# Gated linear attention into two expert layers: the attention output computed turned, with heads on the partitions

## The chip, the cores and the metric

One core of a Trainium2 chip. The metric is the time of one execution on the device, in microseconds (us). The kernel before takes 953.18 us, the median of three runs (951.75 to 960.41).

## What is computed

```python
f = 1.0 / (1.0 + np.exp(-f_logit))
for t in range(S):
    state = f[:, :, t, :, None] * state + np.einsum('bhd,bhe->bhde', k[:, :, t], v[:, :, t])
    y[:, :, t] = np.einsum('bhd,bhde->bhe', q[:, :, t], state)
```

B = 4 sequences, H = 8 heads, S = 768 tokens, D = 48 columns a head. The 3072 tokens with their 384 columns then go through a mixture of 8 experts, of which each token takes two by noisy logits (`x @ w_gate` and `x @ w_noise`), and through a dense layer of 2048 columns with `h - tanh(h)`.

## The kernel before, in words

The attention is done by chunks of 128 tokens, 24 of them: chunk j is part c = j // 4 of sequence b = j % 4. The state of a sequence (`st`, L296) is carried from chunk to chunk, so chunks 0 to 3 have none yet. The loop at the end of the attention part runs over the chunks, and a chunk's work is spread over three turns of it: gates are made three chunks ahead (`decay`), scaled keys and queries two ahead (`scaled`), scores one ahead (`scores`). The order on each engine is the order of the code: `tc.manual_schedule()` is on.

- `scaled` (L314) raises e to the summed log gates for k (`epos`, in SBUF) and to their negative for q (`eneg`), and multiplies: k on the vector engine (DVE, L323), q on GpSimd (POOL, L325). Columns of two heads lie on 128 partitions, 64 a head, four pairs side by side.
- `scores` (L330) multiplies keys and queries on the tensor engine (PE), one head on 64 rows of the array, two heads in turn (`pA`), and DVE masks them into `am`.
- `outputs` (L357) makes the chunk's output with tokens on the partitions: q stationary and the state streaming (L364, 96 columns), scores stationary and v streaming (L366, 48 columns), into `pY`. ScalarE (ACT) copies it twice, as f32 and as scaled f16, and DVE makes the f16 rest.
- `key_rows` (L344) turns keys to rows (`pkr`); `states` (L375) makes the chunk's part of the state (`pK`) and adds it in.
- `x_transposed` (L394) turns the output over (`pE`, three transposes) for `logits` (L406), which multiplies it with 96 columns that begin with the 16 gate and noise columns (`pt`), chunk by chunk.
- `route` (L415) picks experts and slots for a group of four chunks (the last groups: 20 to 22, and 23 alone). It is a generator, `advance` runs it step by step between other work. `post` scatters rows of `xkeep` into the experts' slots in DRAM (`xs`) by GpSimd DMAs.

An f32 product is two passes over the array, each with its own weight load. Behind the loop the experts' products follow (`ph` L185, `py` L200), f16 in two parts, and the dense layer. They aren't touched by the change. The first block of expert 0 starts inside the last turn of the loop; its second block needs all rows scattered.

Of the kernel before, what the change touches and what calls it, by code (L numbers as in the profile page):

```python
# [22 lines left out]
NCH = S // 128  # L23
NT = B * NCH
CAP = 832
GN = 3 * 16 + NT * NE
# [45 lines left out]
def fast(ctx, tc, flag, f_cols, kq_cols, v_rows, gates, blank, w12, w_in, w_out, out):  # L72
# [49 lines left out]
    pre = consts.tile([128, NT + 1, NE], BF, name="pre")  # L122
# [127 lines left out]
    with ExitStack() as actx:  # L250
# [35 lines left out]
        wgn = gn[:, 0:48].rearrange("p (a c) -> p a c", a=3)  # L286
        nz = gn[:, 48:].rearrange("p (c b e) -> p c b e", c=NCH, b=B)
# [69 lines left out]
        def outputs(j):  # L357
            c, b = divmod(j, B)
            am, qT, vt = T.pop(("am", j)), T.pop(("qT", j)), T["v", j]
            pY = ps.tile([128, 512], F32, name="pY", tag="b5")  # L360
            for a in range(4):
                at = 96 * a
                if c:
                    nc.tensor.matmul(pY[:, at:at + 96], qT[:, a, :], st[b][:, at:at + 96], start=True, stop=False)  # L364
                for s in range(2):
                    nc.tensor.matmul(pY[:, at + 48 * s:at + 48 * s + 48], am[:, s, a, :], vt[:, 2 * a + s, :],  # L366
                                     start=not c, stop=bool(s) or not c)
            x = work.tile([128, DM], F32, name="x")
            nc.scalar.activation(x, pY[:, :384], AF.Copy)
            x16 = xkeep[j // 4 % 3][:, j % 4, :]  # L370
            nc.scalar.activation(x16[:, :DM], pY[:, :384], AF.Copy, scale=SX)
            nc.vector.scalar_tensor_tensor(x16[:, DM:], x, SX, x16[:, :DM], op0=OP.mult, op1=OP.subtract)
            T["x", j], T["x16", j] = x, x16

        def states(j):  # L375
            c, b = divmod(j, B)
            vt = T.pop(("v", j))
            if c == NCH - 1:
                return
            k = T.pop(("krows", j))  # L380
            pK = ps.tile([128, 4, 96], F32, name="pK", tag="b6")
            for a in range(4):
                nc.tensor.matmul(pK[:, a, :], k[:, a, :], vt[:, 2 * a:2 * a + 2, :].rearrange("p h d -> p (h d)"),  # L383
                                 start=True, stop=True)
            tsum = work.tile([128, 4, 96], F32, name="tsum")
            if c:
                nc.vector.tensor_tensor(tsum, pK, st[b][:, :384].rearrange("p (a d) -> p a d", a=4), op=OP.add)
            else:
                nc.vector.tensor_copy(tsum, pK)
            nc.gpsimd.tensor_tensor(st[b][:, :384].rearrange("p (a s d) -> p a s d", a=4, s=2),  # L390
                                    tsum.rearrange("p a (s d) -> p a s d", s=2),
                                    gall[:, j, :, :, None].to_broadcast([128, 4, 2, D]), op=OP.mult)
# [22 lines left out]
        def route(g):  # L415
# [25 lines left out]
            for _ in range(2 if g < len(groups) - 2 else 1):  # L441
                yield
            pos = ps.tile([128, 4, NE], F32, name="pt", tag="b7" if g > 4 else "b2")[:, :G]
            nc.tensor.matmul(pos, before, sel[:, jj], start=True, stop=False)
            nc.tensor.matmul(pos, ones, pre[:, jj], start=False, stop=True)
# [60 lines left out]
        for j in range(NT):  # L506
# [24 lines left out]
            x_transposed(j)  # L531
# [3 lines left out]
            if 4 <= j < 20 and not j % 2:  # L535
                split_weights(0, (j - 4) // 2)
        moe_first(*moe_steps[1])
        advance(20)
        post(8)
        logits(NT - 1)  # L540
        chains.append(route(len(groups) - 1))
# [204 lines left out]
    def checks():  # L746
# [9 lines left out]
        nc.tensor.matmul(count[:, 0], ones, pre[:, NT], start=True, stop=True)  # L756
        nc.tensor.matmul(count[:, 1], ones, pre[:, EARLY], start=True, stop=True)
        nc.tensor.matmul(count[:, 2], ones, pre[:, 4], start=True, stop=True)
# [316 lines left out]
def packed_rows(q, k, v, f_logit, w_gate, w_noise, noise, w1, w2):  # L1075
# [11 lines left out]
    gates = np.empty((128, GN), w_gate.dtype)  # L1087
    wgn = gates[:, 0:48].reshape(128, 3, 16)
    wgn[:, :, 0:8] = w_gate.reshape(3, 128, NE).transpose(1, 0, 2)
    wgn[:, :, 8:16] = w_noise.reshape(3, 128, NE).transpose(1, 0, 2)  # L1090
    gates[:, 0:48] = wgn.reshape(128, 48)
    gates[:, 48:] = noise.reshape(B, NCH, 128, NE).transpose(2, 1, 0, 3).reshape(128, NT * NE)
# [30 lines left out]
```

## Time and profile before

| | |
|---|---|
| median of three runs | 953.18 us |
| the profiled execution | 957.17 us |
| its span | 955.4 us |
| mean granted clock of PE | 0.995 of 2.4 GHz |
| PE busy | 940.5 us |
| DVE / ACT / POOL busy | 607.8 / 610.8 / 156.7 us |

The attention loop takes about the first 158 us of the span. Times in the rows are us from the span's start unless marked ns. PE is the product itself, PEld its weight load, which may run beside another product. A row of a timeline gives start, length, engine, line, operation, out<-in, shape and count; in brackets stands the time that the engine was idle before, and who ended it. Ends of products are modelled, so prices are better read from starts.

### The profile page before, as it was taken

Reading aid. Unit: us, or ns where it says so; the run is one execution under the profiler, and the core shown is the slowest. Engines: PE = TensorE matmul, PEld = TensorE weight load, DVE = VectorE, ACT = ScalarE, POOL = GpSimd, SP = SyncE. Lnnn points to the kernel's source line nnn. Section 1 sums busy time; section 2 is a strip of 40 time slices with the busy share of each in tenths; the row PEclk is TensorE's granted clock in tenths of the full one; section 3 lists DMA queues with packets and bytes.
Section 4 is the critical chain, followed back from the end, with each engine's and each line's share of the span. In section 5 each row is a group of like instructions: output and inputs, shape, how many; then the busy total and the mean of one; then the engine's idle time right before and its main releaser. Section 6 shows DMA issues by size and latency. Waiting matters only on the chain.

```text
span 955.4 us, 16329 instructions
## 1 busy us (share of the span) xinstructions
PE 940.5 (98%) x5970; PEld 581.3 (61%) x5970; DVE 607.8 (64%) x1274; ACT 610.8 (64%) x1593; POOL 156.7 (16%) x194
## 2 busy tenths in 40 slices
PE   8999999999999999999999999999999999999996
PEld 8999987555656565555556554555555555555553
DVE  7999995366565556566666655656566565665664
ACT  6777763475757566585858556666666666666653
POOL 2377785200000000000000035200301101000000
PEclk9999998999999999999999999999999999999999
DMA  7877754675464646564554376202222121110001
GB/s 274 282 246 262 251 181 141 179 203 175 139 172 134 186 138 196 138 171 127 153 139 128 95 182 141 67 25 51 75 49 51 34 59 42 42 26 1 34 1 38
DMA packets 111802, 120.04 MB, mean 126 GB/s; under 512 B 66400, under 2 KB 89568, under 8 KB 111584
## 3 DMA queue, kind: packets, MB, share of 16 engines
q1 hardware_dynamic: 105280, 99.63, 36.2%
q0 software_dynamic: 6144, 18.88, 6.4%
q8 instruction: 49, 0.80, 0.4%
q14 instruction: 41, 0.34, 0.1%
q10 hardware_dynamic: 288, 0.39, 0.1%
HBM read 76.41 MB, written 29.88 MB: 111 GB/s over the span
## 4 chain that ended last, share of the span: by engine, by line
PE 94%; DVE 2%; issue 1%; ACT 1%; DMA 1%; POOL 1%; SPq 0%; DVEq 0%; POOLq 0%; ACTq 0%
PE py L200 40%; PE ph L185 39%; PE pY L366 4%; PE pA L339 2%; PE pY L364 2%; PE pK L383 2%; PE pt L410 2%; PE pkr L352 1%; PE pK L492 1%; POOL xs L479 1%; PE pE L398 1%; DMA xt<-xs 0%; DMA xs<-xkeep,yslot 0%; DVE am L341 0%; DVE fc L312 0%
## 5 line engine op out<-in xcount | busy, mean ns | idle before, releaser
L200 PE MATMUL py<-wsplit,hs 128*128 128x384 f16 x2432 | 431.9, 326 | 1.0 <-DVE hs L650 0.8
L200 PEld LDWEIGHTS <-hs 128*128 128x128 f16 x2432 | 237.6, 98 | 172.4 <-DVE hs L650 1.5
L185 PE MATMUL ph<-xt,wsplit 128*128 128x512 f16 (+3 forms) x1152 | 224.4, 340 | 0.8 <-DMA xt<-xs 0.8
L185 PE MATMUL ph<-xt,winS 128*128 128x512 f16 x864 | 201.6, 379 | 0.0
L185 PEld LDWEIGHTS <-wsplit 128*128 128x128 f16 x1152 | 113.0, 98 | 87.6 <-DMA xt<-xs 1.2
L641 DVE SCALAR_TENSOR_TENSOR s<-s,z 128x512 f32<-128x512 f32 x96 | 66.4, 692 | 143.1 <-ACT s L638 142.0
L218 DVE SCALAR_TENSOR_TENSOR hs<-ph,hs 128x256 f16<-128x256 f32 (+2 forms) x192 | 79.7, 443 | 119.3 <-ACT hs L210 112.8
L210 ACT ACTIVATE hs<-ph 128x512 f16<-128x512 f32 (+3 forms) x128 | 65.8, 514 | 133.3 <-PE ph L185 125.3
L608 POOL DMA_INDIRECT g<-y_rows,yslot x48 | 47.8, 996 | 579.4 <-ACT wsplit L144 375.7
L637 ACT ACTIVATE z<-ph 128x512 f32<-128x512 f32 x96 | 57.2, 596 | 131.3 <-PE ph L185 131.3
L185 PEld LDWEIGHTS <-winS 128*128 128x128 f16 x864 | 84.5, 98 | 91.9
L145 DVE SCALAR_TENSOR_TENSOR wsplit<-raw,wsplit 128x768 f16<-128x768 f32 x72 | 70.3, 976 | 16.7 <-ACT wsplit L144 15.5
L149 ACT ACTIVATE junk<-wsplit 128x384 f16<-128x384 f16 x144 | 74.4, 517 | 2.3
L638 ACT ACTIVATE s<-z,bias_a 128x512 f32<-128x512 f32 x96 | 69.3, 722 | 3.1
L643 DVE SCALAR_TENSOR_TENSOR g<-s,ph 128x512 f32<-128x512 f32 x96 | 65.9, 687 | 3.3
L650 DVE TENSOR_TENSOR hs<-g,hs 128x512 f16<-128x512 f32 x96 | 65.7, 684 | 0.1
L144 ACT ACTIVATE wsplit<-raw 128x768 f16<-128x768 f32 x72 | 59.9, 832 | 1.3 <-DMA raw<-wo_f 1.3
L649 ACT ACTIVATE hs<-g 128x512 f16<-128x512 f32 x96 | 58.9, 613 | 1.1 <-DVE g L643 1.1
L479 POOL DMA_INDIRECT xs<-xkeep,yslot x48 | 56.1, 1169 | 18.8 <-issue 9.1
L366 PE MATMUL pY<-v,am 128*128 128x48 f32 x384 | 55.0, 272 | 0.0
L366 PEld LDWEIGHTS pY<-v,am 128*128 128x128 f32 x384 | 51.4, 198 | 0.1
L325 POOL TENSOR_TENSOR kqT<-eneg,kq 128x512 f32<-128x512 f32 x23 | 32.6, 1419 | 16.7 <-ACT eneg L321 16.4
(135 smaller groups left out, 910.1 us busy)
## 6 DMA issues: line engine op xcount, KB each, us to landing
raw<-in_w SPq DMA_DIRECT2D x64, 384.0 KB
kq<-in_kq_cols SPq DMA_DIRECT2D x24, 512.0 KB
y_rows<-yo SPq DMA_DIRECT2D x47, 192.0 KB
f<-in_f_cols SPq DMA_DIRECT2D x24, 256.0 KB
w<-in_moe_w_out SPq DMA_DIRECT2D x32, 192.0 KB
w<-in_moe_w_in SPq DMA_DIRECT2D x24, 256.0 KB
v<-in_v_rows SPq DMA_DIRECT2D x24, 192.0 KB
out<-o SPq DMA_DIRECT2D x22, 192.0 KB
```

The source lines that it names most:

```text
L145: nc.vector.scalar_tensor_tensor(t[:, 1], raw, SW, t[:, 0], op0=OP.mult, op1=OP.subtract)
L149: nc.scalar.activation(junk[:, :DM], RING[e, f][:, 0, 3 * i:3 * i + 3, :].rearrange("p a b -> p (a b)"), AF.Square, accum_out=wsum[:, 8 * ...
L185: nc.tensor.matmul(ph[:, :n], l, x[:, r, :n], start=(o == 0), stop=(o == 8))
L200: nc.tensor.matmul(p[:max(m, 128)], l, r, start=(f == 0 and o == 0), stop=(f == last and o == len(ops) - 1))
L210: nc.scalar.activation(hs[:, :n], ph[:, :n], AF.Relu, accum_out=hacc[:, at:at + 1])
L218: nc.vector.scalar_tensor_tensor(hs[:, at:at + hi - lo], ph[:, lo:hi], 0.0, hs[:, lo:hi], op0=OP.max, op1=OP.subtract)
L366: nc.tensor.matmul(pY[:, at + 48 * s:at + 48 * s + 48], am[:, s, a, :], vt[:, 2 * a + s, :], start=not c, stop=bool(s) or not c)
L479: sc = nc.gpsimd.indirect_dma_start(out=xs, out_offset=bass.IndirectOffsetOnAxis(ap=yslot[:, r, j:j + 1], axis=0), in_=T["x16", j], in_off ...
L638: nc.scalar.activation(s, z, AF.Square, scale=1.0 / SZ, bias=bias_a)
L641: nc.vector.scalar_tensor_tensor(s, s, ZD, z, op0=OP.add, op1=OP.mult)
L643: nc.vector.scalar_tensor_tensor(g, s, 0.5, ph, op0=OP.mult, op1=OP.mult)
L650: nc.vector.tensor_tensor(hs[:, 512:], g, hs[:, :512], op=OP.subtract)
```

## The change

The output of a chunk is made with heads' columns on the partitions and tokens in the free dimension: the state and v are stationary, q and the masked scores stream. The state gets 64 columns a head, with zeros behind the 48, so that the output of a pair of heads fills the partitions in the same padded layout as q. The products of v write 48 partitions, from 0 or from 64. ACT copies the turned output once, into a tile for the group's four chunks; four transposes turn it back to rows, which are split to f16 in the next turn. The logits of a group are one product: 16 gate columns stationary, 512 tokens streaming, and four small transposes bring them to rows. In the last group (one chunk) they are made as before. The counts for the slots are kept per group, and the product that makes slots adds up the chunks of a group. e to the gates for k is written to PSUM.

```diff
-GN = 3 * 16 + NT * NE
+GN = 4 * 16 + NT * NE
...
-        wgn = gn[:, 0:48].rearrange("p (a c) -> p a c", a=3)
+        wgn = gn[:, 0:64].rearrange("p (a c) -> p a c", a=4)
...
-        st = [acst.tile([128, 432], F32, name=f"st{b}") for b in range(B)]
+        st = [acst.tile([128, 4, 2, 64], F32, name=f"st{b}") for b in range(B)]
         for s_ in st:
-            nc.vector.memset(s_[:, 384:], 0.0)
+            nc.gpsimd.memset(s_, 0.0)
...
-            epos = work.tile([128, 512], F32, name="epos", bufs=1)
+            epos = ps.tile([128, 512], F32, name="epos", tag="b2")
...
         def outputs(j):
-            pY = ps.tile([128, 512], F32, name="pY", tag="b5")
+            pY = ps.tile([128, 4, 128], F32, name="pY", tag="b5")
+            if not c:
+                nc.tensor.matmul(pY, none, ones[:, None, :].to_broadcast([128, 4, 128]), start=True, stop=False)
+            else:
+                for a in range(4):
+                    nc.tensor.matmul(pY[:, a, :], st[b][:, a].rearrange("p s d -> p (s d)"), qT[:, a, :], start=(a == 0),
+                                     stop=False)
             for a in range(4):
-                at = 96 * a
-                if c:
-                    nc.tensor.matmul(pY[:, at:at + 96], qT[:, a, :], st[b][:, at:at + 96], start=True, stop=False)
                 for s in range(2):
-                    nc.tensor.matmul(pY[:, at + 48 * s:at + 48 * s + 48], am[:, s, a, :], vt[:, 2 * a + s, :],
-                                     start=not c, stop=bool(s) or not c)
-            x = work.tile([128, DM], F32, name="x")
-            nc.scalar.activation(x, pY[:, :384], AF.Copy)
-            x16 = xkeep[j // 4 % 3][:, j % 4, :]
-            nc.scalar.activation(x16[:, :DM], pY[:, :384], AF.Copy, scale=SX)
-            nc.vector.scalar_tensor_tensor(x16[:, DM:], x, SX, x16[:, :DM], op0=OP.mult, op1=OP.subtract)
-            T["x", j], T["x16", j] = x, x16
+                    nc.tensor.matmul(pY[64 * s:64 * s + D, a, :], vt[:, 2 * a + s, :], am[:, s, a, :], start=False,
+                                     stop=(a == 3))
+            g = group_of[j]
+            if j == groups[g][0]:
+                T["yT", g] = work.tile([128, 4, 4, 128], F32, name="yT")
+            nc.scalar.activation(T["yT", g][:, :, j - groups[g][0], :], pY, AF.Copy)
...
-        def x_transposed(j):
-            x = T.pop(("x", j))
-            p = ps.tile([128, 3, 128], F32, name="pE", tag="b0")
-            for a in range(3):
-                nc.tensor.transpose(p[:, a, :], x[:, a * 128:(a + 1) * 128], ident)
-            xT = work.tile([128, 3, 128], F32, name="xT", bufs=1)
-            nc.scalar.activation(xT, p, AF.Copy)
-            T["xT", j] = xT
+        def x_rows(j):
+            g = group_of[j]
+            p = T["pX", j] = ps.tile([128, 4, 128], F32, name="pX", tag="b0")
+            for a in range(4):
+                nc.tensor.transpose(p[:, a, :], T["yT", g][:, a, j - groups[g][0], :], ident)
+
+        def x_split(j):
+            p = T.pop(("pX", j)).rearrange("p a (s d) -> p (a s) d", s=2)[:, :, :D]
+            x16 = T["x16", j] = xkeep[j // 4 % 3][:, j % 4, :]
+            hi, lo = (x16[:, i * DM:(i + 1) * DM].rearrange("p (h d) -> p h d", h=H) for i in range(2))
+            nc.scalar.activation(hi, p, AF.Copy, scale=SX)
+            nc.vector.scalar_tensor_tensor(lo, p, SX, hi, op0=OP.mult, op1=OP.subtract)
...
-        def logits(j):
+        def logits(g):
+            y = T["yT", g]
             p = ps.tile([128, 96], F32, name="pt", tag="b7")
-            xT = T.pop(("xT", j))
-            for a in range(3):
-                nc.tensor.matmul(p, xT[:, a, :], gn[:, 16 * a:16 * a + 96], start=(a == 0), stop=(a == 2))
-            nc.scalar.activation(lgs[:, j, :], p[:, :16], AF.Copy)
+            for a in range(4):
+                nc.tensor.matmul(p, y[:, a, 0, :], gn[:, 16 * a:16 * a + 96], start=(a == 0), stop=(a == 3))
+            nc.scalar.activation(lgs[:, groups[g][0], :], p[:, :16], AF.Copy)
+
+        def group_logits(g):
+            G = len(groups[g])
+            p = ps.tile([16, 4, 128], F32, name="pt", tag="b7")
+            for a in range(4):
+                nc.tensor.matmul(p[:, :G], wgn[:, a, :], T["yT", g][:, a, :G, :], start=(a == 0), stop=(a == 3))
+            t = T["lgT", g] = work.tile([16, 4, 128], F32, name="lgT", bufs=1)
+            nc.scalar.activation(t[:, :G], p[:, :G], AF.Copy)
+
+        def group_rows(g):
...
+            for i in range(G):
+                nc.tensor.transpose(p[:, i, :], t[:, i, :], ident[:16, :16])
+            nc.scalar.activation(lgs[:, j0:j0 + G, :], p[:, :G], AF.Copy)
...
-            for j in js:
+            yield
+            if G > 1:
+                own_sum = small.tile([128, NE], BF, name="own_sum")
...
+                    nc.vector.tensor_reduce(own_sum, sel[:, jj].rearrange("p g e -> p e g"), axis=AX.X, op=OP.add)
...
+            tt(pre[:, g + 1], pre[:, g], own_sum, op=OP.add)
+            for _ in range(5 if g < len(groups) - 2 else 1):
                 yield
-                tt(pre[:, j + 1], pre[:, j], sel[:, j], op=OP.add)
...
-            nc.tensor.matmul(pos, ones, pre[:, jj], start=False, stop=True)
+            for i in range(1, G):
+                nc.tensor.matmul(pos[:, i:], ones, sel[:, j0 + i - 1, None, :].to_broadcast([128, G - i, NE]),
+                                 start=False, stop=False)
+            nc.tensor.matmul(pos, ones, pre[:, g, None, :].to_broadcast([128, G, NE]), start=False, stop=True)
...
             if j:
-                logits(j - 1)
+                x_split(j - 1)
                 if j - 1 in ends:
-                    chains.append(route(group_of[j - 1]))
+                    group_logits(group_of[j - 1])
             advance(rate)
             outputs(j)
+            if j - 1 in ends:
+                group_rows(group_of[j - 1])
+                chains.append(route(group_of[j - 1]))
             advance(rate)
             if last:
                 moe_first(*moe_steps[0])
+                logits(len(groups) - 1)
+                chains.append(route(len(groups) - 1))
             key_rows(j + 1)
             advance(rate)
             states(j)
-            x_transposed(j)
+            x_rows(j)
```

Left out: the same renumbering in the checks at the end and in the host's packing (gate weights padded as the heads are), the zero tile `none`, and `tsum` reading the padded state.

PE in a chunk inside a group (chunk 18), from the state's product to the turning. Before:

```order
L364 MATMUL pY<-st_160,kqT 128x96
L366 MATMUL pY<-v,am 128x48 x2
L364 MATMUL pY<-st_160,kqT 128x96
L366 MATMUL pY<-v,am 128x48 x2
L364 MATMUL pY<-st_160,kqT 128x96
L366 MATMUL pY<-v,am 128x48 x2
L364 MATMUL pY<-st_160,kqT 128x96
L366 MATMUL pY<-v,am 128x48 x2
L352 MATMUL pkr<-ident,kqT 128x128 x4
L383 MATMUL pK<-v,krows 128x96 x4
L398 MATMUL pE<-ident,x 128x128 x3
```

With the change:

```order
L367 MATMUL pY<-kqT,st_162 128x128 x4
L371 MATMUL pY<-am,v 48x128 x8
L354 MATMUL pkr<-ident,kqT 128x128 x4
L386 MATMUL pK<-v,krows 128x96 x4
L402 MATMUL pX<-ident,yT 128x128 x4
```

Twelve products of pY that alternate became four with the state (`st`) and then eight with v; the turning has four transposes and reads the turned copy. The logits' product that stood behind pA in each chunk is gone from here.

PE in the chunk behind a group's end (chunk 16), from the last score product on. Before:

```order
L339 MATMUL pA_1701<-kqT 128x128
L410 MATMUL pt<-gn,xT 128x96 x3
L364 MATMUL pY<-st_158,kqT 128x96
L366 MATMUL pY<-v,am 128x48 x2
L364 MATMUL pY<-st_158,kqT 128x96
L366 MATMUL pY<-v,am 128x48 x2
```

With the change:

```order
L341 MATMUL pA_1643<-kqT 128x128
L425 MATMUL pt<-yT,gn 16x512 x4
L367 MATMUL pY<-kqT,st_160 128x128 x4
L371 MATMUL pY<-am,v 48x128 x8
L435 MATMUL pt<-ident,lgT 128x16 x4
L354 MATMUL pkr<-ident,kqT 128x128 x4
L386 MATMUL pK<-v,krows 128x96 x4
```

Here the group's four products of 512 columns (L425) stand ahead of pY, and the four small transposes (L435) behind it.

PE in the last chunk, from the transposes of chunk 22 to the experts' first product. Before:

```order
L398 MATMUL pE<-ident,x 128x128 x3
L410 MATMUL pt<-gn,xT 128x96 x3
L364 MATMUL pY<-st_161,kqT 128x96
L366 MATMUL pY<-v,am 128x48 x2
L364 MATMUL pY<-st_161,kqT 128x96
L366 MATMUL pY<-v,am 128x48 x2
L364 MATMUL pY<-st_161,kqT 128x96
L366 MATMUL pY<-v,am 128x48 x2
L364 MATMUL pY<-st_161,kqT 128x96
L366 MATMUL pY<-v,am 128x48 x2
L185 LDWEIGHTS wsplit
```

With the change:

```order
L371 MATMUL pY<-am,v 48x128 x8
L402 MATMUL pX<-ident,yT 128x128 x4
L425 MATMUL pt<-yT,gn 16x384 x4
L367 MATMUL pY<-kqT,st_163 128x128 x4
L371 MATMUL pY<-am,v 48x128 x8
L435 MATMUL pt<-ident,lgT 128x16 x3
L187 LDWEIGHTS wsplit
```

Ahead of the last pY stand now four products of 384 columns, which read copies made in earlier chunks. Before it was chunk 22's own logits, behind its transposes and their copy.

## Rows read from the trace of the kernel before

**Rows 1.** The page, part 1: busy time of each engine.

```profile
PE 940.5 (98%) x5970; PEld 581.3 (61%) x5970; DVE 607.8 (64%) x1274; ACT 610.8 (64%) x1593; POOL 156.7 (16%) x194
```

**Rows 2.** Stretches: length, busy PE, PEld, DVE, ACT, POOL; clock, DMA share, GB/s.

```profile
67.00:73.20 6.20, 6.20 (x65) 5.91 (x64) 6.10 (x16) 4.85 (x12) 5.46 (x6) 1.00 0.76 247
...
155.00:160.00 5.00, 5.00 (x24) 4.15 (x24) 0.55 (x3) 0.87 (x2) 4.04 (x8) 0.50 0.43 160
```

**Rows 3.** Timeline of PE over one chunk, 65 to 72.

```profile
65.09 0.49 PE L398 MATMUL pE<-ident,x 128*128 128x128 f32 x3
65.51 1.16 PE L339 MATMUL pA<-kqT 64*128 64x128 f32 x16
66.61 0.91 PE L410 MATMUL pt<-gn,xT 128*128 128x96 f32 x6
67.35 0.39 PE L364 MATMUL pY<-st,kqT 128*128 128x96 f32 x2
...
69.99 0.18 PE L444 MATMUL pt<-sel,before 128*128 128x32 bf16 x1
...
70.05 0.63 PE L352 MATMUL pkr<-ident,kqT 128*128 128x128 f32 x4
70.52 1.03 PE L383 MATMUL pK<-v,krows 128*128 128x96 f32 x8
71.38 0.49 PE L398 MATMUL pE<-ident,x 128*128 128x128 f32 x3
```

**Rows 4.** Weight loads (PEld) and the product that follows each, narrow windows, 66 to 68.

```profile
67.83 0.19 PEld L366 LDWEIGHTS pY<-v,am 128*128 128x128 f32 x1
...
67.87 0.28 PE L366 MATMUL pY<-v,am 128*128 128x48 f32 x1
...
66.71 0.19 PEld L410 LDWEIGHTS pt<-gn,xT 128*128 128x128 f32 x1
...
66.79 0.61 PE L410 MATMUL pt<-gn,xT 128*128 128x96 f32 x4
...
66.06 0.31 PEld L339 LDWEIGHTS pA<-kqT 64*128 64x128 f32 x4
...
66.17 0.50 PE L339 MATMUL pA<-kqT 64*128 64x128 f32 x6
```

**Rows 5.** Groups of instructions, 35.9 to 129.3 (15 chunks): busy, mean ns, idle before.

```profile
L341 DVE TENSOR_TENSOR am<-pA,tri 128x512 f32<-128x512 f32 x30 | 19.2, 681 | 2.9 <-PE pA L339 2.9
...
L323 DVE SCALAR_TENSOR_TENSOR kqT<-epos,kq 128x512 f32<-128x512 f32 x15 | 15.3, 1018 | 0.0
...
L479 POOL DMA_INDIRECT xs<-xkeep,yslot x26 | 32.8, 1260 | 4.8 <-issue 4.8
L325 POOL TENSOR_TENSOR kqT<-eneg,kq 128x512 f32<-128x512 f32 x15 | 21.9, 1459 | 2.6 <-ACT eneg L321 2.6
L390 POOL TENSOR_TENSOR st<-tsum,gall 128x384 f32<-128x384 f32 x14 | 11.7, 834 | 18.3 <-DVE pre L440 10.5 <-DVE yslot L464 7.7
```

**Rows 6.** Timeline at the end of the loop and behind it, DVE and PE.

```profile
136.98 3.18 DVE L323 SCALAR_TENSOR_TENSOR kqT<-epos,kq 128x512 f32<-128x512 f32 x1
...
140.30 1.16 PE L339 MATMUL pA<-kqT 64*128 64x128 f32 x16 [0.66 <-DVE gall L326]
...
151.48 0.55 PE L398 MATMUL pE<-ident,x 128*128 128x128 f32 x3 [0.58 <-ACT x L369]
152.67 0.91 PE L410 MATMUL pt<-gn,xT 128*128 128x96 f32 x6 [0.64 <-ACT xT L400]
153.41 0.56 PE L364 MATMUL pY<-st,kqT 128*128 128x96 f32 x2
...
158.39 2.58 PE L185 MATMUL ph<-xt,wsplit 128*128 128x384 f16 x9
...
161.22 1.63 PE L185 MATMUL ph<-xt,wsplit 128*128 128x384 f16 x9
...
182.28 1.88 PE L185 MATMUL ph<-xt,wsplit 128*128 128x448 f16 x9 [0.84 <-DMA xt<-xs]
```

More of the change, by code (lines that the diff above doesn't have):

```diff
@@ L121, in fast @@
     sel = consts.tile([128, NT, NE], BF, name="sel")
-    pre = consts.tile([128, NT + 1, NE], BF, name="pre")
+    pre = consts.tile([128, 8, NE], BF, name="pre")
+    none = consts.tile([128, 128], BF, name="none")
+    nc.vector.memset(none, 0.0)
     nc.vector.memset(pre[:, 0, :], 0.0)
@@ L386, in states @@
             if c:
[L387 removed]
+                nc.vector.tensor_tensor(tsum.rearrange("p a (s d) -> p (a s) d", s=2),
+                                        pK.rearrange("p a (s d) -> p (a s) d", s=2),
+                                        st[b].rearrange("p a s d -> p (a s) d")[:, :, :D], op=OP.add)
             else:
                 nc.vector.tensor_copy(tsum, pK)
[L390 to L391 removed]
+            nc.gpsimd.tensor_tensor(st[b][:, :, :, :D], tsum.rearrange("p a (s d) -> p a s d", s=2),
                                     gall[:, j, :, :, None].to_broadcast([128, 4, 2, D]), op=OP.mult)
[L394 to L401 removed]
+        def x_rows(j):
[9 more added lines that the diff above has]
+            nc.vector.scalar_tensor_tensor(lo, p, SX, hi, op0=OP.mult, op1=OP.subtract)
         groups = [[4 * g + i for i in range(4)] for g in range(5)] + [[20, 21, 22], [23]]
@@ L405, in fast @@
         group_of = {j: g for g, js in enumerate(groups) for j in js}
-        def logits(j):
+        def logits(g):
+            y = T["yT", g]
             p = ps.tile([128, 96], F32, name="pt", tag="b7")
-            xT = T.pop(("xT", j))
-            for a in range(3):
-                nc.tensor.matmul(p, xT[:, a, :], gn[:, 16 * a:16 * a + 96], start=(a == 0), stop=(a == 2))
-            nc.scalar.activation(lgs[:, j, :], p[:, :16], AF.Copy)
+            for a in range(4):
[9 more added lines that the diff above has]
+        def group_rows(g):
+            G = len(groups[g])
+            j0 = groups[g][0]
+            t = T.pop(("lgT", g))
+            p = ps.tile([128, 4, 16], F32, name="pt", tag="b7")
+            for i in range(G):
+                nc.tensor.transpose(p[:, i, :], t[:, i, :], ident[:16, :16])
+            nc.scalar.activation(lgs[:, j0:j0 + G, :], p[:, :G], AF.Copy)
         scatters = []
@@ L437, in route @@
             tt(oh, nl, m8[:, :G, 0:1].to_broadcast([128, G, NE]), op=OP.is_equal)
-            for j in js:
+            yield
+            if G > 1:
+                own_sum = small.tile([128, NE], BF, name="own_sum")
+                with nc.allow_low_precision("counts up to 24"):
+                    nc.vector.tensor_reduce(own_sum, sel[:, jj].rearrange("p g e -> p e g"), axis=AX.X, op=OP.add)
+            else:
+                own_sum = sel[:, j0]
+            yield
+            tt(pre[:, g + 1], pre[:, g], own_sum, op=OP.add)
+            for _ in range(5 if g < len(groups) - 2 else 1):
                 yield
-                tt(pre[:, j + 1], pre[:, j], sel[:, j], op=OP.add)
-            for _ in range(2 if g < len(groups) - 2 else 1):
-                yield
-            pos = ps.tile([128, 4, NE], F32, name="pt", tag="b7" if g > 4 else "b2")[:, :G]
+            pos = ps.tile([128, 4, NE], F32, name="pt", tag="b7")[:, :G]
             nc.tensor.matmul(pos, before, sel[:, jj], start=True, stop=False)
-            nc.tensor.matmul(pos, ones, pre[:, jj], start=False, stop=True)
+            for i in range(1, G):
+                nc.tensor.matmul(pos[:, i:], ones, sel[:, j0 + i - 1, None, :].to_broadcast([128, G - i, NE]),
+                                 start=False, stop=False)
+            nc.tensor.matmul(pos, ones, pre[:, g, None, :].to_broadcast([128, G, NE]), start=False, stop=True)
             tt(dv[:, jj], m8[:, :G, 1], m8[:, :G, 0], op=OP.subtract)
@@ L536, in fast @@
                 split_weights(0, (j - 4) // 2)
+        x_split(NT - 1)
         moe_first(*moe_steps[1])
@@ L539, in fast @@
         post(8)
-        logits(NT - 1)
-        chains.append(route(len(groups) - 1))
         advance(3)
@@ L755, in checks @@
         count = ps.tile([128, 3, NE], F32, name="pt", tag="b7")
-        nc.tensor.matmul(count[:, 0], ones, pre[:, NT], start=True, stop=True)
-        nc.tensor.matmul(count[:, 1], ones, pre[:, EARLY], start=True, stop=True)
-        nc.tensor.matmul(count[:, 2], ones, pre[:, 4], start=True, stop=True)
+        nc.tensor.matmul(count[:, 0], ones, pre[:, 7], start=True, stop=True)
+        nc.tensor.matmul(count[:, 1], ones, pre[:, EARLY // 4], start=True, stop=True)
+        nc.tensor.matmul(count[:, 2], ones, pre[:, 1], start=True, stop=True)
         total = consts.tile([128, 3], F32, name="total")
@@ L1086, in packed_rows @@
     kq = np.concatenate([by_head(t, 0.0) for t in (k, q)], axis=2)
[L1087 to L1092, printed above, removed]
+    gates = np.zeros((128, GN), w_gate.dtype)
+    wgn = np.zeros((2, 64, 4, 16), w_gate.dtype)
+    for w, at in ((w_gate, 0), (w_noise, NE)):
+        wgn[:, :D, :, at:at + NE] = w.reshape(4, 2, D, NE).transpose(1, 2, 0, 3)
+    gates[:, 0:64] = wgn.reshape(128, 64)
+    gates[:, 64:] = noise.reshape(B, NCH, 128, NE).transpose(2, 1, 0, 3).reshape(128, NT * NE)
     w12 = np.empty((NE * 8, 128, 2 * DM), w1.dtype)
```

2 lines of the change are left out of this document (1 added, 1 removed).

## Prediction

> **What bounds the kernel now.** I read the page first: TensorE (PE) is busy for 98% of the span [rows 1]. So time is won or lost almost only where PE's own list gets shorter or longer. Then the table by stretches: in a chunk of the attention loop (67.0 to 73.2) PE is busy 6.20 us of 6.20, VectorE (DVE) 6.10, GpSimd (POOL) 5.46 and ScalarE (ACT) 4.85 [rows 2]. PE is the bound, but DVE and POOL are close behind: if PE's list got much shorter, they would take over. Then PE's timeline of one chunk, because its start times give the price of each kind of product [rows 3], and single records of weight loads and products, because they tell whether the load or the stream sets a product's price [rows 4]. Last the end of the attention loop, the only place where PE waits [rows 6].
>
> Prices from [rows 3], by differences of starts. An f32 product goes over the array twice (24 passes for the 12 products of pY). pY: 67.35 to 69.99, 2.64 us for 24 passes, 0.11 a pass, although its passes stream 96 or 48 columns. pK: 8 passes in 0.86, 0.11. pkr: 4 transposes in 0.47. So a pass over the whole array with 128 f32 weight columns costs 0.11 whatever it streams: the weight load sets it. pA uses half arrays (64 rows, two heads side by side): 16 passes in 1.10, 0.069 each, so two halves do run abreast. Its edges cost extra: pE before it takes 0.42 for 3 passes (0.33 by price), pt behind it 0.74 for 6 (0.66), together 0.17 for changing the shape of the array and back.
>
> The stream's price is in [rows 4]: a product is recorded after its load by 0.04 us for 48 f32 columns, 0.08 for 96, 0.11 for 128, which is two clocks a column at the 2.4 GHz level (the granted clock is 1.00 there, rows 2). So 512 f32 columns should take 0.43 us, and 128 columns 0.11, just what a 128-column load takes.
>
> **The change on PE, part by part** (24 chunks; the first four have no state).
> - pY, chunks 4 to 23. Before 24 passes, 2.64. Now 4 products with the state stationary, 8 passes of 128 streamed columns: 0.88. And 8 products with 48 columns of v stationary, 16 passes that stream 128 columns and fill half the array's columns. No row of before shows column halves. From above a pass is bound by 0.11 (no overlap), from below by 0.055 (two streams of 0.11 wholly abreast). I take 0.069, since pA's row halves are the nearest row: 1.10, and 0.17 for the edges. Sum 2.15, so 0.49 less, times 20: **-9.8 us**.
> - pY, chunks 0 to 3. Before 16 passes, 1.76. Now one bf16 product of 512 columns (0.21 at 2.4 GHz), 1.10 and 0.17: 0.28 less, times 4: **-1.1**.
> - Turning y back to rows takes 4 transposes instead of 3: 0.11 times 24: **+2.6**.
> - Logits. Before 6 passes per chunk, 0.66, times 24: 15.8. Now for each of five groups of four 8 passes that stream 512 columns (8 x 0.43 = 3.43), 4 transposes (0.44) and two more changes of the array's shape (0.34): 4.21, times 5: 21.1. The group of three: 8 x 0.32 + 3 x 0.11 + 0.34 = 3.2. The last chunk alone: 0.88. Sum 25.2: **+9.4**. The price of the 512-column pass lies between 0.215 (one clock a column) and 0.46; I keep both ends for the range.
> - The slots' product becomes five bf16 products instead of two, 0.03 each (69.99 to 70.05 for two): **+0.5**.
>
> So on PE's list the gain of the turned output is eaten by the logits: -10.9 against +12.5, **+1.6 us**. The reason is that the old logits streamed 96 columns behind a 128-column load that had to be paid anyway, while the new ones stream every one of 512 columns at two clocks.
>
> Perfetto Trace Analysis of the Trainium skill (Engine Utilization) halves TensorE's output rate for FP32_LOW_HIGH, and the offsets of rows 4 agree. The skill's page TensorE: Matmul & The Clock Gate (Back-to-back issue gap) gives N/2.4 + 2.5 ns for a warm product, 0.216 us for 512 columns, with no word on f32; by it the five groups' logits would cost 8.6 us less than in my sum (the second rival).
>
> **What goes on the other engines.** k's exp now lands in PSUM, so DVE's product L323 has one operand less in SBUF. It takes 1018 ns on average, beside 681 for am, which reads PSUM and has the same size [rows 5]; once it took 3.18 us, while POOL was busy [rows 6]. I expect 0.68: 0.34 less per chunk. In the loop that is worth nothing, since PE does not wait for DVE there (rows 2). ACT's exp writes PSUM instead of SBUF and the copies out of pY write 512 elements: hidden under ACT's 1.35 us of slack per chunk. DVE's counting per chunk becomes per group: hidden too. POOL now clears the state at the start: four writes, between nothing and 4 x 1.46 (its product of the same size, rows 5), ahead of its first work and beside the first gate and scan; I take 0, at most 1 if DVE's first steps wait for them.
>
> New waits. The four transposes wait for ACT's copy of pY (about 0.6, by 512 elements); up to chunk 18 pkr and pK (1.33) stand between and cover it. The small transposes wait for ACT's copy of the wide logits, covered by pY (2.15). On ACT the copy of pY is queued behind that one, but needs pY, which PE makes later anyway. On DVE the f16 rest waits for ACT's f16 copy, made 1 us earlier in the turn; route's steps and tsum stand behind it. Slots come half a turn later, so in turn 20 five scatters instead of two stand ahead of q's scaling of chunk 23: 3 x 1.44 = 4.3 on POOL, and PE asks for that q two turns (over 9 us) later. All this I count as nothing.
>
> A chunk without logits has 1.10 + 0.08 + 2.15 + 0.47 + 0.86 + 0.53 = 5.19 us of PE work. POOL's list for it is 1.46 + 0.83 and two scatters of 1.26 + 0.18 [rows 5], 5.17, and a short write ahead of each scatter: some 5.3. So three chunks in four would be POOL's by 0.1 us, while the fourth (9.4 us on PE) lets POOL catch up. q's scaling is done two chunks ahead, so POOL may lag: between 0 and 15 x 0.2 = 3. I take **+1.0**.
>
> **The end of the loop** [rows 6]. PE waits 0.66 us for L323 (the 3.18 one; the row's releaser stands behind it on DVE) and 0.64 for xT ahead of the last chunk's logits. Both go: the new logits of chunks 20 to 22 need only the turned copy. The waits of the transposes for ACT's copy (0.58 at 151.48, and two like it) stay and grow by some 0.1 each, as the copy has 512 elements instead of 384. Sum **-1.0**. The granted clock is 0.50, the 1.2 GHz level, from 155 to 160 (rows 2): behind these two waits, which lie 1.2 us apart, the last pY takes 4.98 (153.41 to 158.39) instead of 2.64, and the first nine products of the experts 2.58 instead of 1.63. With the change that stretch is filled: 8 passes of 384 columns, 2.6 us, stand between those transposes and the last pY. I expect the clock to hold at 2.4 GHz: **-3.3**, between 0 and that. Behind it PE waits 0.84, at 182.28, for the transposed rows of the next block. Their chain (last pY, slots, 8 scatters, transfer) gets no shorter. PE's work beside it loses 1.0 by the clock and gains some 0.7 by logits and transposes: **+0.3**.
>
> Sum: +1.6 + 1.0 - 1.0 - 3.3 + 0.3 = -1.4. The profiled execution took 957.17 (span 955.4 and 1.8 around it), 0.4% above the median of 953.18. Against the median that makes 951.8; I say **951.5 us**, no change that can be measured: a run of this kernel tells about 1% from none.
>
> **Rivals.**
> 1. *The two column halves do not run abreast: slower.* Then a pass costs 0.11, 16 of them 1.76: +0.66 per chunk, +15.8, **967 us**. For it: no row shows column halves, and both halves take their rows from the same partitions, unlike pA's. Against: pA's two halves do overlap (0.069). It decides once a pass costs more than 0.098: 384 passes x 0.029 = 11.2, the way to +1%. Chance 0.22.
> 2. *f32 streams at one clock a column, so that rows 4 show something else than the stream: faster.* Then the wide logits cost 8 x 0.215 (-9.9 over all groups), a pair of v's passes 0.055 instead of 0.11 (-0.46 per chunk, -11). A chunk without logits falls to 4.7 and POOL's 5.3 holds it: 15 x 0.6 = 9 come back, -20.9 + 9 from 951.5: **940 us**. Against it: the offsets grow with the columns, 0.04 for 48 and 0.08 for 96. For it: no row has f32 streams that set the pace by themselves. Chance 0.20.
> 3. *The clock still drops at the end, or POOL holds the plain chunks*: +3.3 or +2, 954 to 955. They stay within 1% and are in the forecast's own range, 946 to 958.
>
> That the change does not do what it says I give nothing: PE's list shows each move.
>
> **How the numbers follow.** Forecast 0.58, rival 1 0.22, rival 2 0.20. The range reaches to both rivals, 940 to 968, and leaves out the outer half of each. Faster by over 1% (below 943.6): three quarters of rival 2 and 0.05 of the forecast, 0.20. Slower by over 1% (above 962.7): four fifths of rival 1 and 0.04, 0.22. The rest 0.58.
>
> **What would show it.** In the changed profile: 0.43 between the starts of the wide logits' passes (0.22 would be rival 2); 16 passes of v in about 1.1 (1.8 would be rival 1); pY at 2.15 in all; chunks of 5.2 to 5.4 us and one in four of 9.4; L323 at 0.68; the granted clock at 1.00 through the last chunk; PE still busy 98%. I am wrong if PE waits in the plain chunks for more than 0.3 us each, or if the attention loop ends more than 8 us from 158.4.

## The result and the profile after

The changed kernel takes 961.91 us, the median of 20 runs (959.79 to 962.93). The kernel before, run beside it, takes 956.62 (20 runs, 951.75 to 960.75). The ratio is 1.0054, 95% interval 1.0038 to 1.0070: by the medians the change costs about 5 us. The forecast was 1.4 us less, 951.5 us; the size is small, but the sign is wrong. The kernel before takes longer in runs with a lower granted clock; at equal clock the change costs 10 us (last series below). The span of the profiled execution grew from 955.4 to 960.8 us.

The page, part 1, answers to [rows 1], and two lines of its part 4 follow (the chain of work that ended last, its shares of the span by engine):

```profile
PE 937.8 (98%) x5950; PEld 552.8 (58%) x5950; DVE 595.6 (62%) x1260; ACT 606.1 (63%) x1558; POOL 155.9 (16%) x198
...
PE 88%; DVE 7%; ACT 2%; issue 2%; DVEq 0%
```

PE's busy time fell by 2.7 us, though the span grew by 5.4. So PE's list did not get longer; PE waits more. The chain goes over DVE for 7% of the span, and for 2% in the kernel before, whose line is:

```profile
PE 94%; DVE 2%; issue 1%; ACT 1%; DMA 1%; POOL 1%; SPq 0%; DVEq 0%; POOLq 0%; ACTq 0%
```

PE's timeline over two chunks answers to [rows 3]; chunk 8 carries the logits of chunks 4 to 7:

```profile
60.92 1.16 PE L341 MATMUL pA<-kqT 64*128 64x128 f32 x16
62.01 3.61 PE L425 MATMUL pt<-yT,gn 128*16 128x512 f32 x8
65.55 1.16 PE L367 MATMUL pY<-kqT,st 128*128 128x128 f32 x8
66.64 1.08 PE L371 MATMUL pY<-am,v 128*48 128x128 f32 x16
67.65 0.42 PE L435 MATMUL pt<-ident,lgT 16*128 16x16 f32 x4
68.00 0.66 PE L354 MATMUL pkr<-ident,kqT 128*128 128x128 f32 x4
...
69.89 1.16 PE L341 MATMUL pA<-kqT 64*128 64x128 f32 x16
...
75.64 0.63 PE L402 MATMUL pX<-ident,yT 128*128 128x128 f32 x4 [0.83 <-DVE xkeep L409]
76.19 1.16 PE L341 MATMUL pA<-kqT 64*128 64x128 f32 x16
```

By differences of starts: the 16 passes of v take 1.01 us, the state's 8 take 1.09 with the edge, pY 2.10 in all (forecast 2.15), and a pass of the wide logits 3.54 / 8 = 0.44 (forecast 0.43). Rival 1 (halves that don't run abreast, 1.76) and rival 2 (0.22 a pass) are both out. But pX waits: 0.83 us at 75.64, for DVE's f16 rest. The table of PE's waits, from 12 us to the end of the loop (total, times, longest):

```profile
PE pX L402 <- DVE xkeep L409: 8.0, 12, 0.9
...
PE pX L402 <- DVE sr L496: 1.2, 4, 0.3
```

Here lie 9.2 us that the forecast doesn't have (`sr`, a short step of route, stands right behind the rest on DVE). The chain shows how one such wait comes about (start, duration, what):

```profile
77.53 1.28 DVE am L343 x2
78.80 0.60 DVE kqT L325
...
79.47 1.13 DVE fc L314
80.61 0.45 DVE xkeep L409
81.06 0.08 DVE sr L496
...
81.20 0.63 PE pX L402 x4
81.83 1.14 PE pA L341 x16
...
83.56 0.68 DVE am L343
84.24 0.60 DVE kqT L325
...
84.97 1.13 DVE fc L314
86.10 0.46 DVE xkeep L409
...
86.70 0.63 PE pX L402 x4
```

The rows show a ring. pX(j) needs the one PSUM bank that pX(j-1) holds until DVE has read it for the f16 rest (`xkeep`, L409). That rest stands on DVE behind the mask (`am`), the k product and the scan (`fc`) of the same turn. `am` needs pA, and pA stands on PE right behind the last pX. Once round takes 86.70 - 81.20 = 5.50 us; PE's own work in such a chunk is less. In the kernel before the bank of pE was freed by ACT's copy `xT`, in no such ring.

From the start of one pA to the next a group of four chunks takes 8.97, 6.30, 5.57 and 5.50 us, together 26.3; the forecast had 25.3 (9.4 and three times 5.3). The last pY ends at 162.04 instead of 158.39 [rows 6], +3.65 us. From there to the next block's first product 26.86 us pass (188.90) instead of 23.89 (182.28): another +2.97. The rest of the program takes 771.9 us instead of 773.1. PE's timeline behind the loop answers to [rows 6]:

```profile
162.32 1.64 PE L187 MATMUL ph<-xt,wsplit 128*128 128x384 f16 x9
...
169.61 0.18 PE L475 MATMUL pt<-sel,before 128*128 128x8 bf16 x1 [2.01 <-DVE sel L461]
...
169.67 2.40 PE L187 MATMUL ph<-xt,wsplit 128*128 128x384 f16 x9
171.87 2.58 PE L202 MATMUL py<-wsplit,hs 128*128 128x384 f16 x9
174.28 1.63 PE L187 MATMUL ph<-xt,wsplit 128*128 128x384 f16 x9
...
188.90 1.87 PE L187 MATMUL ph<-xt,wsplit 128*128 128x448 f16 x9
```

The clock held through the last chunk, as forecast: the first nine expert products take 1.64 us, where before they took 2.58 [rows 6]. In this profile it fell later instead. The slots' product of the last chunk (L475) is now ahead of the third expert product on PE and waits 2.01 us for the picks; behind that wait the next 18 products take 4.61 us instead of 2.92, and the granted clock of 170 to 175 is 0.66 on average. The wait belongs to the change, the fall to this execution: five other profiles below have the wait and no fall, one of them of this same kernel.

### The profile page after: what moved, and what is told of

The parts are those of the page before. It is cut to its first block, busy times and chain, and to the rows that moved or that the text cites. A ratio compares the mean times of both kernels' runs of the same rounds, so it can differ in the third digit from the quotient of the medians.

```text
span 960.8 us, 16249 instructions
## 1 busy us (share of the span) xinstructions
PE 937.8 (98%) x5950; PEld 552.8 (58%) x5950; DVE 595.6 (62%) x1260; ACT 606.1 (63%) x1558; POOL 155.9 (16%) x198
## 3 DMA queue, kind: packets, MB, share of 16 engines
q1 hardware_dynamic: 105280, 99.64, 35.9%
## 4 chain that ended last, share of the span: by engine, by line
PE 88%; DVE 7%; ACT 2%; issue 2%; DVEq 0%
PE py L202 41%; PE ph L187 40%; PE pt L425 2%; DVE fc L314 2%; PE pA L341 2%; DVE am L343 1%; PE pX L402 1%; DVE kqT L325 1%; PE pK L526 1%; PE pY L367 1%; DVE xkeep L409 1%; PE pY L371 1%; ACT yT L376 0%; DVE tsum L390 0%; DVE pr L491 0%
## 5 line engine op out<-in xcount | busy, mean ns | idle before, releaser
L513 POOL DMA_INDIRECT xs<-xkeep,yslot x48 | 51.6, 1074 | 15.5 <-issue 9.1
L343 DVE TENSOR_TENSOR am<-pA,tri 128x512 f32<-128x512 f32 x48 | 30.8, 684 | 12.3 <-PE pA L341 12.1
L376 ACT ACTIVATE yT<-pY 128x512 f32<-128x512 f32 x24 | 14.3, 596 | 27.1 <-PE pY L371 25.6
```

## The experiments

Theory A: the ring costs what the forecast lacks. Theory B: the new products are the longer list, and the waits only show slack. All kernels start from the changed one unless another is named. Each ratio is against the kernel before, run on the same chip; the first four kernels share a chip, the next four another, the last four a third.

**Split first.** The split goes to the start of the turn, ahead of `scores`.

```diff
             rate = 4 if last else 2
+            if j:
+                x_split(j - 1)
             scores(j + 1)
...
-            if j:
-                x_split(j - 1)
-                if j - 1 in ends:
-                    group_logits(group_of[j - 1])
+            if j - 1 in ends:
+                group_logits(group_of[j - 1])
```

> The split of chunk j-1 (ACT's f16 copy, DVE's f16 rest) is issued at the start of turn j, ahead of the products of scores, and no longer behind them and the scan. Theory A (the one bank of pX comes free only behind DVE's am, kqT, gall and scan, so that pX, scores, am, kqT, scan and the rest close a ring of about 5.5 us around 5.1 us of products): the waits of pX for the rest, 8.0 us in 12 instructions, fall below 2 us, the loop ends 5 to 8 us earlier, 953 to 957 us. Theory B (the products themselves are the longer list now, wide logits above all; the waits only show slack that would come out elsewhere): the waits move to another product (pA or pY for DVE), time within 1.5 us of 961.

Measured 951.75 us (949.86 to 952.44), ratio 0.9953 (0.9934 to 0.9972): 10 us under the changed kernel, below A's 953 to 957, and by the medians faster than the kernel before. First its chain of waits over plain chunks (start, duration, what), in which PE now stands alone, then PE's waits over the same time as above:

```profile
65.67 1.09 PE pA L341 x16
66.76 1.09 PE pY L367 x8
67.85 1.01 PE pY L371 x16
70.96 1.09 PE pA L341 x16
...
76.04 1.09 PE pA L341 x16
```

```profile
PE pt L475 <- DVE sel L461: 2.6, 2, 2.0
PE pX L402 <- ACT yT L376: 1.5, 3, 0.7
...
PE pA L341 <- POOL spacer L512: 1.1, 1, 1.1
```

pX waits for DVE no more. The slots' product still waits 2.0 us, but here the clock of 160 to 165 is 1.00. From the second group on, a group takes 8.97, 5.29, 5.08 and 5.08: the three plain chunks lose 1.01, 0.49 and 0.42, the chunk with the wide product nothing, as A has it. The first chunks, which have no state, fall from 5.44 to 4.32. The last pY ends at 152.73, 9.3 us earlier. A expected 5 to 8; it left out the first chunks.

**Two banks.** pX alternates between two banks; k's exponentials make room in SBUF.

```diff
-            epos = ps.tile([128, 512], F32, name="epos", tag="b2")
+            epos = work.tile([128, 512], F32, name="epos", bufs=1)
...
-            p = T["pX", j] = ps.tile([128, 4, 128], F32, name="pX", tag="b0")
+            p = T["pX", j] = ps.tile([128, 4, 128], F32, name="pX", tag=("b0", "b2")[j % 2])
```

> pX takes two PSUM banks in turn, and the exponentials for k go back to SBUF to make room for the second. Theory A: the product no longer waits for the rest of the chunk before, the waits of pX go to under 1 us and the loop ends 5 to 8 us earlier, less what the slower k product (1.02 instead of 0.68 us on DVE) costs: 953 to 957 us. Theory B: within 1.5 us of 961.

Measured 951.75 us, ratio 0.9956 (0.9937 to 0.9975). The order on DVE is the changed kernel's, only the bank is another, and from the second on the groups again take 8.97, 5.29, 5.08 and 5.08. pX waits 2.0 us, all of it for ACT's copy, where A had under 1; the time is below A's range here too. Two different cuts of the ring, one in the order, one in the bank, give the same time. Theory B is out.

**Exponentials in SBUF alone** (the first of these two edits).

> The exponentials for k go back to SBUF alone, one bank for pX as in the kernel after. Theory A: the k product, 0.34 us longer, stands in the ring of 5.5 us, so each of some 20 turns is up to 0.34 us longer: plus 4 to 7 us, 965 to 968 us. Theory B, in which DVE doesn't bound the turns: within 1.5 us of 961.

Measured 963.34 us, ratio 1.0088 (1.0057 to 1.0119). By the medians that is 1.4 us above the changed kernel, not A's 4 to 7, and above B's range as well; the intervals of the two ratios overlap. The price that A assumed was wrong: DVE and POOL in its timeline show it.

```profile
85.31 1.27 POOL L327 TENSOR_TENSOR kqT<-eneg,kq 128x512 f32<-128x512 f32 x1
...
86.15 0.97 DVE L325 SCALAR_TENSOR_TENSOR kqT<-epos,kq 128x512 f32<-128x512 f32 x1
...
90.12 1.27 POOL L327 TENSOR_TENSOR kqT<-eneg,kq 128x512 f32<-128x512 f32 x1
...
91.89 0.68 DVE L325 SCALAR_TENSOR_TENSOR kqT<-epos,kq 128x512 f32<-128x512 f32 x1
```

From SBUF the k product takes 0.97 us beside POOL's q product and 0.68 alone, and its median over 24 is 0.68. From the second on the groups take 8.97, 6.31, 5.58 and 5.74: one chunk in four is longer, by 0.24; only three chunks ahead of that lose more, 0.4 to 1.2 each, and the longest of them (6.71) is 6.69 in the repeat of the changed kernel too. So this run says little about the ring.

**Late slots.** The last chunk's logits and route go back to their place of before, behind `post(8)`.

```diff
                 moe_first(*moe_steps[0])
-                logits(len(groups) - 1)
-                chains.append(route(len(groups) - 1))
...
         post(8)
+        logits(len(groups) - 1)
+        chains.append(route(len(groups) - 1))
         advance(3)
```

> The logits and slots of the last chunk go back to where the kernel before has them, behind the second group of expert products and the scatters. Theory A (the route of the last chunk now starts so early that its products' waits for DVE stand ahead of the third expert product on PE: 2.0 us and then half the clock for 2 groups): the 2 us wait is gone, the stretch from the last pY to the second block's first product is 23.9 us as before, minus 2.5 to 4 us: 957 to 959 us, the loop itself unchanged. Rival (that stretch is bound by the scatters and the loads behind them, or the wait is one that moves): within 1 us of 961.

Measured 960.37 us, ratio 1.0047 (1.0027 to 1.0066). The loop ends as in the changed kernel (last pY at 162.00), the 2.01 us wait and the fall of the clock are gone (another wait, for the slots of chunks 20 to 22, is 1.43 instead of 0.56):

```profile
165.34 0.19 PE L475 MATMUL pt<-sel,before 128*128 128x24 bf16 x1 [1.43 <-DVE sel L461]
...
171.48 0.18 PE L475 MATMUL pt<-sel,before 128*128 128x8 bf16 x1
...
171.55 1.62 PE L187 MATMUL ph<-xt,wsplit 128*128 128x384 f16 x9
...
186.38 1.88 PE L187 MATMUL ph<-xt,wsplit 128*128 128x448 f16 x9
```

The next block starts 24.38 us behind the last pY, 2.5 less than 26.86. But 1.7 of that is the fall of the clock (4.61 - 2.92), which the repeat of the changed kernel does not have; it needs 25.18 us there, 0.8 more than here. The time lies in the rival's range (within 1 us of 961), not in A's 957 to 959, and the intervals overlap: the wait goes with the late slots, what it is worth in time is not shown.

**Logits per chunk.** The wide product goes; each chunk makes its logits in the form that the last one has.

```diff
             if j:
                 x_split(j - 1)
+                logits(j - 1)
                 if j - 1 in ends:
-                    group_logits(group_of[j - 1])
+                    chains.append(route(group_of[j - 1]))
...
-            if j - 1 in ends:
-                group_rows(group_of[j - 1])
-                chains.append(route(group_of[j - 1]))
```

> The wide product and its transposes go; each chunk makes its own logits from its own turned output (4 products of 8 passes with 96 columns, as the last chunk of the kernel after does), right after the products of scores. The split and the one bank of pX stay as in the kernel after. Theory A (a ring of 5.5 us that only the chunks without the wide product are short enough to feel): the products of every turn are now about 5.1 + 0.9 = 6.0 us, longer than the ring, so the ring hides again: four turns about 24.1 instead of 26.3 us, the waits of pX below 2 us, 949 to 954 us. Theory B (the ring would show under any list): the waits of pX stay near 8 us and the time within 3 us of 961.

Measured 959.17 us, ratio 1.0000 (0.9978 to 1.0023): 0.5% better than the changed kernel by the ratios, but short of A's 949 to 954. In the loop A held: with bank and order untouched, three chunks in four take 5.97 us and the fourth 6.1 to 6.5, and pX waits for the rest three times, 1.1 us in all. Longer products cover the ring. The last pY ends 7.5 us earlier than in the changed kernel, but what was gained was lost behind it: 

```profile
159.18 0.60 ACT L376 ACTIVATE yT<-pY 128x512 f32<-128x512 f32 x1 [5.15 <-remote]
...
159.82 2.03 PE L419 MATMUL pt<-gn,yT 128*128 128x96 f32 x8 [3.01 <-ACT yT L376]
```

ACT stood 5.15 us for what the profile only calls "remote", PE waited 3.01 for it, and the products behind ran at the lower clock (0.50 from 160 to 165). Later, in the dense layer, ACT stood another 6.5 us for "remote"; from the next block's first product (183.40) to the end this profile takes 776.5 us, the changed kernel 771.9. All four kernels of this chip have such a wait (3.7 us or more), and so has the profile of the kernel before (4.9), but none of the eight kernels on the other two chips, nor the changed kernel. What it is was not tried; it blurs the times of this series, and whether logits per chunk alone would be faster without it stays open.

**Split first with late slots** (the first and the fourth diff together).

> The early split and the late slots together. If the two losses are separate, the gains add: 951.75 - 1.5 = 950 us, 949 to 951.5. If the early split already took the wait that the late slots take, 951.75 as with the early split alone.

Measured 959.26 us, ratio 0.9993 (0.9970 to 1.0016): neither of the two expected values. Up to chunk 20 its chunks are those of the early split; then ACT's `yT` waits 3.7 us for "remote", and the clock falls twice. It was run again below.

**The kernel before with k's exponentials in PSUM** and nothing else changed.

```diff
-            epos = work.tile([128, 512], F32, name="epos", bufs=1)
+            epos = ps.tile([128, 512], F32, name="epos", tag="b2")
...
-            pos = ps.tile([128, 4, NE], F32, name="pt", tag="b7" if g > 4 else "b2")[:, :G]
+            pos = ps.tile([128, 4, NE], F32, name="pt", tag="b7")[:, :G]
```

> The kernel before with one part of the change alone: the exponentials for k in a PSUM bank (positions go to the bank of the logits). The k product on DVE falls from 1.02 or more to 0.68 us. In the kernel before the products bound the turns, so the forecast's term of nothing holds if the time is within 1.5 us of before; a gain of 3 us or more would say that DVE bounded its turns.

Measured 958.02 us, ratio 1.0011 (0.9989 to 1.0033): no difference that can be told. The k product takes 0.675 to 0.693 us in every chunk, and the chunks stay at 6.22: PE set them, as the forecast said.

**All three:** split first, late slots, logits per chunk (the three diffs together).

> Early split, late slots and logits per chunk together. Per turn 0.9 us of logits stand against (4.2 + 0.35)/4 = 1.1 us for the wide product with its transposes, so with the ring gone the turns' products are 0.1 to 0.2 us shorter: 2 to 4 us below the early split with late slots, 946 to 948 us; if POOL's scatters bound the turns (two scatters, the q product and the state, some 5.3 us), no gain in the last turns, 949 to 951 us.

Measured 952.43 us, ratio 0.9934 (0.9914 to 0.9954), with the "remote" wait of this chip in it (4.8 us); the 946 to 948 expected were missed. The chunks take 5.97 and one in four 6.1, 24.0 a group against 24.4 with the wide product.

**The last series on one chip.** Split first with logits per chunk (two of the diffs above), the last slots early:

> The early split with logits per chunk, the last chunk's logits and slots early as in the kernel after. If the wide product's only fault is its length (1.1 against 0.9 us a chunk), 2 to 4 us less than the early split alone, ratio to before 0.991 to 0.993. If the scatters and the transposed loads behind them already bound the end of the loop with the early split, the same ratio as the early split alone, 0.995.

Measured **945.58 us** (944.96 to 946.93), ratio 0.9896 (0.9854 to 0.9939): the best kernel, by the medians 11 us under the one before and 16 under the changed one, and 6 under the early split alone, where 2 to 4 or nothing were expected. Its rows:

```profile
69.55 1.16 PE L341 MATMUL pA<-kqT 64*128 64x128 f32 x16
70.64 1.13 PE L419 MATMUL pt<-gn,yT 128*128 128x96 f32 x8
71.61 1.08 PE L367 MATMUL pY<-kqT,st 128*128 128x128 f32 x8
...
75.52 1.16 PE L341 MATMUL pA<-kqT 64*128 64x128 f32 x16
...
153.04 0.18 PE L459 MATMUL pt<-sel,before 128*128 128x8 bf16 x1 [0.29 <-DVE sel L445]
...
171.71 1.88 PE L187 MATMUL ph<-xt,wsplit 128*128 128x448 f16 x9 [0.90 <-DMA xt<-xs]
```

A chunk's logits take 0.97 from start to start, four of them 3.88; the wide product with its small transposes takes 3.89. So the logits themselves gain nothing. A group is 24.0 against 24.4 us, since the state's passes take 1.01 behind the logits and 1.09 behind pA. More comes at the end: with no wide product ahead of the last chunk, the last pY ends at 148.25; with the split first alone, on this chip, it ends at 153.45 (some 1.5 us of it from a fall of the clock in that profile). And the route is so far on that its last wait is 0.29 us instead of 2.02. The next block then waits 0.90 for its transposed rows: the scatters or the transfer behind them come next there.

Split first alone, the first diff:

> The early split once more, beside the early split with late slots and the kernel after on one chip. Theory A: 0.995 of before and 9 to 11 us under the kernel after.

Measured 951.69 us, ratio 0.9953 (0.9929 to 0.9977): the same as on the first chip.

Split first with late slots:

> The early split with late slots once more. If the late slots lose in themselves when the loop ends early (products of the expert layer wait for slots of chunks 20 to 22, then half the clock), it stays 3 to 5 us above the early split on this chip too; if the first pair was apart only because it ran on two chips, the two agree within 1 us.

Measured 950.91 us, ratio 0.9935 (0.9910 to 0.9960). On this chip, with no "remote" wait, it agrees with the early split within 1 us; the late slots are no loss, and with the early split hardly a gain.

The changed kernel without an edit:

> The kernel after, unchanged, as the measure for the other three on this chip: 1.0054 of before.

Measured 962.04 us, ratio 1.0063 (1.0036 to 1.0089). So on one chip, from the changed kernel to the split moved up: 10.35 us less. The wait for the slots is there again, but the clock holds behind it:

```profile
170.50 0.18 PE L475 MATMUL pt<-sel,before 128*128 128x8 bf16 x1 [2.01 <-DVE sel L461]
...
170.56 1.62 PE L187 MATMUL ph<-xt,wsplit 128*128 128x384 f16 x9
```

This series also shows what the clock does to the comparison. The runs of the kernel before go from 951.81 us at a mean granted clock of 0.998 to 965.23 at 0.982. Its seven runs at 0.997 and 0.998 average 952.8; at these clocks the changed kernel averages 962.9 (seven runs) and the early split 952.1 (eight). So at equal clock the change costs 10 us, about twice what the medians show, and the early split is level with the kernel before; its lead in the medians lies in the clock. Split first with logits per chunk stays ahead: 946.4 at 0.998 against 952.1.

## Why the prediction was wrong

- **The step that failed** is the one that lists the new waits: "On DVE the f16 rest waits for ACT's f16 copy, made 1 us earlier in the turn; route's steps and tsum stand behind it", and then "All this I count as nothing". It names what is queued behind the rest on DVE, but not what is queued ahead of it (mask, k product, scan, which hang on pA), nor who waits for it: pX, by its one bank. Two cuts of that ring take 10 us off; the missing term is that large. The text and the trace of before have the prices: pX 0.53, pA 1.10, two masks 1.36, k product 0.68 as expected there, scan 1.21 and rest 0.53 are 5.4 us, near the 5.50 measured, against 5.19 of PE work in the same text. Scan and rest in the kernel before:

```profile
82.61 1.21 DVE L312 TENSOR_TENSOR_SCAN fc<-carry,fc 128x512 f32<-128x512 f32 x1
83.74 0.53 DVE L372 SCALAR_TENSOR_TENSOR xkeep<-x,xkeep 128x384 f16<-128x384 f32 x1
```

- **The rival that was not there.** The text says that the forecast is wrong "if PE waits in the plain chunks for more than 0.3 us each". It does (up to 0.9), and each chunk is longer by 0.4 to 1.0 than without the ring. The rivals were about prices of products, and there the forecast held. (In rival 2, eight pairs of v's passes at 0.055 less each are -0.44 a chunk, not -0.46.)
- **PE's list: right, a little too dear.** pY 2.10 (2.15), wide pass 0.44 (0.43), 16 passes of v 1.01 (1.10). The wide logits with their transposes came to 3.54 + 0.35 = 3.89 instead of 4.21, since the small transposes with their changes of the array's shape cost less. With the ring cut the plain chunk is 5.08 where the text had 5.19. TensorE: Matmul & The Clock Gate of the Trainium skill (Back-to-back issue gap) would give 0.216 us for the wide pass; the trace disagrees for f32, and the measurement decides.
- **k's exponentials: right.** 0.68 us in every chunk, and worth nothing alone (ratio 1.0011).
- **POOL's +1.0: right in size, not in place.** With the ring cut, PE waits for POOL (`spacer`, the short write ahead of a scatter) once near the loop's end, 1.1 us, and not in three chunks of four; 1.4 us at the loop's start are in the kernel before as well, though the text calls the loop's end the only place where PE waits.
- **The clock's -3.3: right.** It held through the last chunk, and all 20 runs of the changed kernel have a mean clock of 0.997 to 0.999, where the kernel before went down to 0.982 in the last series. In one profile 1.7 of it was lost again behind the slots' wait of 2.01 us. But the forecast took the 3.3 off a median of three runs, 953.18, that probably had little of it to lose: in the last series runs of the kernel before near 953 are at 0.997.
- **The route of the last chunk: overlooked.** The forecast looked at the transfer to the next block ("+0.3") and not at the route of the last chunk, which the change put ahead of PE's third expert product. That step measured +2.97, and +1.3 in the repeat, where the clock held; the late slots take 0.8 of that.
- **The sum.** Without the clock the forecast was +1.9. At equal clock the early split, which has no ring but still the slots' wait, measured -0.7, that is 2.6 less, as the products were cheaper than priced. The ring took 10.8 away: +10. The clock, forecast at -3.3, gave some 5 back between the medians: +5.3.

## What to carry to other kernels

When a buffer's last reader moves to another engine, ask where that reader stands in the new engine's queue, what the work ahead of it waits for, and whether that leads back to the writer. If it does, add up the ring and compare it with the bound engine's work per turn; one bank more, or the reader first in the queue, cuts it. And merging small products into a rare big one makes the other turns short: what the long turns hid shows in the short ones.

## What the runs showed of the hardware

A DVE product with both operands in SBUF takes 0.68 us alone, 0.97 where a POOL product of the same size runs beside it (both in the run with the exponentials in SBUF alone), and 3.18 once in the kernel before; with one operand in PSUM it took 0.675 to 0.693 in all 48 cases of the changed kernel and of the kernel before with only that edit. SBUF — State Buffer of the Trainium skill (Who interferes with whom) says that DVE and GpSimd exclude each other when a DVE instruction has two SBUF inputs and the GpSimd one reads SBUF; these rows agree.

Half the array's columns, two streams in turn, run abreast as row halves do: 16 passes of 48 weight columns and 128 streamed columns in 1.01 us, 0.063 each, where two passes one behind the other would take 0.11 each. An f32 pass of 512 columns behind a 16-column load takes 0.44 us at the 2.4 GHz level.

The same wait of PE, 2.0 us ahead of the slots' product, was followed by a fall of the granted clock in one profile (0.66 from 170 to 175) and by none in five others, of which one is of the same kernel.
